# Filter rows of two groups loaded ahead into the space of matrices that are done with, in a spectral-filter kernel on Trainium2

**Chip, cores, metric.** One core of a Trainium2 chip; different calls used different chips. The metric is the device time of one execution in microseconds (us), median of several runs. All times "at 41.72" are microseconds from the start of the profiled execution's span.

## The reference, cut to what matters

```python
# x: 2048 x 1024 bf16; w_r, w_i: 2048 x 513 bf16 (the filter, real and imaginary part)
def _A_ref(x, w_r, w_i):                       # spectral layer
    X = rfft2(x.astype(float32))
    X = X * (w_r + 1j * w_i)
    return irfft2(X, s=(S, D)).astype(bfloat16)

def _B_ref(x, w1, b1, w2): ...                 # feed-forward layer 1024 -> 3584 -> 1024, mish

x = x + _A_ref(_layernorm(x), A_w_r, A_w_i)    # the early loads touch only this line
x = x + _B_ref(_layernorm(x), B_w1, B_b1, B_w2)
x = x + _A_ref(_layernorm(x), A_w_r, A_w_i)
x = x + _B_ref(_layernorm(x), B_w1, B_b1, B_w2)
```

## The kernel before

The Fourier transforms are matmuls with DFT tables. The spectral layer runs in steps over 8 groups of rows (two halves each): a first step `s1` with scaled matrices, a second (`s2`) and third (`s3`) forward, two inverse ones (`i1`, `i2`), a round trip through memory (`u_turn`, `u_back`, `u_last`) that transposes, and a fifth step after it. The steps of different groups are interleaved by the list in `order_A` (a word such as `241` is step 2, group 4, half 1).

Before `s3` can multiply group g by the filter, that group's filter rows (512 KB: `w_r` and `w_i`, 256 KB each) must be in SBUF, and `filter_bins(g)` must have arranged them: four matmuls (L921) that mirror the bins, two VectorE copies (L932) and two ScalarE copies (L936). In the first spectral layer (`li == 0`) the rows lie in a ring `WR` of two buffers, so group g+2 may only be loaded when group g has been used up:

```python
self.o = dict(..., WR=54 * K, YS=96 * K, UT=64 * K, MN=64 * K, ...)   # bytes in each partition
# ... cut
def load_w(self, g):
    if self.li == 0:
        self.load_wr(self.WR[g % 2], g)
        return
# ... cut: the second layer reads back what the first has arranged
def load_wr(self, wr, g):
    wr.res.begin()                     # waits for all readers of what lay in the buffer
    a, b = slots_of(g)
    for c, src in enumerate((self.w_r, self.w_i)):
        rows = src.rearrange("(k s) d -> k s d", s=16)[:, a:b + 1:b - a, 1:513]
        self.dma(self.sp if g < 2 else self.pool, wr.ap[:, c, :, :], rows, ..., parts=[wr.res])
```

```python
self.s1(li)                            # reads the scaled matrices at offset MN
# ... cut: the rings of the later steps
self.UT = self.alloc("UT", o["UT"], [P, P])      # the transposed components, over the same space
self.r_ut = self.sub_res(self.UT, "ut", 4, o["UT"], P * P * 2)
for r in self.r_ut:
    r.begin()
for stage, g, h in self.order_A():
    if stage == 2:
        s2(g, h)
        if li == 0 and h == 0:
            filter_bins(g)
            if g < 6:
                load_w(g + 2)
    elif stage == 3:
        s3(g, h)
        if h:
            if g < 6:
                load_tabs(g + 2)       # forward table c_ft
            # ... cut
    elif stage == 4:
        i1(g, h)
        if h and g < 6:
            load_btabs(g + 2)          # inverse table c_bt
    else:
        i2(g, h)
        u_turn(g, h)
self.spin(26, 0)                       # filler matmuls while the round trip ends
```

`UT` and `MN` have the same offset: the scaled matrices are read for the last time in `s1`, and the transposed components arrive only when the first `u_back` runs, tens of microseconds later. In between, the space is empty, but it already belongs to `UT`.

## Time and profile before

| | before |
|---|---|
| median of 3 runs (lowest to highest) | 1017.54 us (1015.78 to 1019.77) |
| span of the profiled execution, granted clock | 1016.2 us, 0.998 |
| TensorE / ScalarE / VectorE busy over the span | 94% / 34% / 32% |
| stage touched: first second-step matmul to last inverse step | 39.67 to 105.20 us |

The averages over the span are mostly those of the feed-forward layers. What the change is worth is read in the stage alone, from the timelines of single engines: each line is start, length, engine, source line, operation and shapes, count, and in a bracket the idle time just before and what ended it. The prediction below shows most of these lines. The GpSimd timeline, with the issue of the `w_r` part for group 2 and for group 6:

```profile
41.72 0.77 POOL L249 DMA_DIRECT2D ARENA<-in_A_w_r_dram  x1 [3.97 <-PE PS L921]
...
68.72 0.71 POOL L249 DMA_DIRECT2D ARENA<-in_A_w_r_dram  x1 [7.01 <-PE PS L697]
```

The ScalarE timeline around TensorE's wait for group 2 (the line between these two, at 49.21, is in the prediction):

```profile
47.66 1.13 ACT L732 ACTIVATE ARENA<-PS 128x1024 bf16<-128x1024 f32 x1
...
50.07 1.02 ACT L749 ACTIVATE ARENA<-PS 128x1024 bf16<-128x1024 f32 x1
```

A transfer that nobody waits for costs nothing. The first GpSimd line is where group 2's rows are asked for, and the second is one that I call **the hinge**: everything that stands behind it in the GpSimd queue, above all the inverse table `c_bt`, starts no sooner.

### The profile page before, as it was taken

How to read it: one execution, taken by the hardware profiler on the slowest of the kernel's cores; microseconds unless marked ns; L12 is line 12 of the kernel's file. 1: busy time of each engine (PE TensorE's matmuls, PEld its weight loads, DVE VectorE, ACT ScalarE, POOL GpSimd, SP SyncE). 2: the span in 40 equal slices, each digit the busy share in tenths (PEclk: the TensorE clock that was granted, in tenths of full speed). 3: DMA queues.
4: the chain of work that ended last, by engine and by line, in shares of the span. 5: the costliest groups of instructions: out<-in, count | busy, mean ns of one | idle time of the engine just before them, and what ended most of it. 6: DMA issues, size and time to landing. Idle time of an engine off the chain costs nothing.

```text
span 1016.2 us, 13732 instructions
## 1 busy us (share of the span) xinstructions
PE 955.1 (94%) x5779; PEld 507.3 (50%) x5865; DVE 326.5 (32%) x679; ACT 347.3 (34%) x482; POOL 81.5 (8%) x114
## 2 busy tenths in 40 slices
PE   0799799999999999999999978999999999999998
PEld 0577575444444444444456757644444444444443
DVE  6797469002444000033347736830011100000111
ACT  7798384330000433300029847543100024330000
POOL 4651000000000000002511100000000000000000
PEclk9999999999999999999999999999999999999999
DMA  9979813562111220002932875246411212100000
GB/s 283 247 221 320 212 61 114 181 205 72 47 46 32 73 83 21 1 21 82 195 66 82 233 188 140 89 156 207 126 27 46 73 52 80 45 1 11 21 26 27
DMA packets 154205, 107.00 MB, mean 105 GB/s; under 512 B 74448, under 2 KB 133664, under 8 KB 154144
## 3 DMA queue, kind: packets, MB, share of 16 engines
q1 hardware_dynamic: 143056, 78.61, 27.3%
q0 software_dynamic: 8912, 25.84, 8.8%
q10 hardware_dynamic: 2176, 1.66, 0.5%
q8 instruction: 47, 0.77, 0.3%
q14 instruction: 14, 0.11, 0.0%
HBM read 80.85 MB, written 20.71 MB: 100 GB/s over the span
## 4 chain that ended last, share of the span: by engine, by line
PE 86%; DVE 4%; DMA 4%; ACT 4%; issue 1%; SPq 0%; POOL 0%; ACTq 0%; DVEq 0%; POOLq 0%
PE PS L1057 38%; PE PS L1040 37%; PE PS L771 2%; PE PS L697 2%; PE PS L792 2%; DMA ARENA<-c_bt 1%; PE PS L950 1%; ACT ARENA L441 1%; DMA ARENA<-u_scratch 1%; DVE ARENA L619 1%; DMA XS<-in_A_x_dram 1%; ACT ARENA L550 1%; PE PS L1006 1%; DVE ARENA L592 1%; PE PS L810 1%
## 5 line engine op out<-in xcount | busy, mean ns | idle before, releaser
L1040 PE MATMUL PS<-ARENA 128*128 128x512 bf16 (+1 forms) x1950 | 389.3, 358 | 2.5 <-DVE ARENA L1011 0.6
L1057 PE MATMUL PS<-ARENA 128*128 128x512 bf16 x1756 | 385.5, 379 | 1.9
L1044 ACT ACTIVATE ARENA<-PS,B 128x512 bf16<-128x512 f32 (+1 forms) x248 | 158.9, 645 | 410.9 <-PE PS L1040 410.6
L1040 PEld LDWEIGHTS PS<-ARENA 128*128 128x128 bf16 x1984 | 192.8, 98 | 193.8 <-DVE ARENA L1011 1.5
L1057 PEld LDWEIGHTS PS<-ARENA 128*128 128x128 bf16 x1792 | 175.4, 98 | 211.4
L1062 DVE TENSOR_TENSOR XS<-PS,XS 128x512 bf16<-128x512 f32 x64 | 44.2, 691 | 587.1 <-PE PS L1057 587.1
L460 DVE BATCH_NORM_STATS2 BN<-XS 128x6 f32<-128x512 bf16 x100 | 64.7, 675 | 6.2 <-DMA XS<-in_A_x_dram 5.0
L550 ACT ACTIVATE ARENA<-PS 128x1440 bf16<-128x1440 f32 (+3 forms) x26 | 28.0, 1095 | 28.0 <-DVE XS L972 24.4
L249 POOL DMA_DIRECT2D xn_scratch<-ARENA x12 | 6.5, 541 | 374.5 <-DVE ARENA L512 374.5
L771 PE MATMUL PS<-ARENA 128*128 128x256 bf16 x256 | 32.4, 273 | 4.1 <-DVE ARENA L760 3.2
L778 ACT ACTIVATE ARENA<-PS 128x1024 bf16<-128x1024 f32 x32 | 33.0, 1051 | 7.1 <-PE PS L771 7.1
L432 ACT ACTIVATE RS<-MV,EPS 128x2 f32<-128x2 f32 (+2 forms) x5 | 1.5, 298 | 96.8 <-DVE MV L463 96.2
L697 PE MATMUL PS<-FD,ARENA 128*128 128x256 bf16 (+1 forms) x256 | 31.8, 271 | 2.4 <-ACT ARENA L617 1.2
L749 ACT ACTIVATE ARENA<-PS 128x1024 bf16<-128x1024 f32 x32 | 32.5, 1044 | 4.5 <-PE PS L745 4.5
L771 PEld LDWEIGHTS PS<-ARENA 128*128 128x128 bf16 x256 | 24.2, 98 | 11.8 <-DVE ARENA L760 5.5
L753 DVE TENSOR_TENSOR ARENA<-ARENA 128x1024 bf16<-128x1024 bf16 x32 | 22.0, 688 | 20.4 <-ACT ARENA L749 20.3
L697 PEld LDWEIGHTS PS<-FD,ARENA 128*128 128x128 bf16 x256 | 24.4, 98 | 6.5 <-DVE ARENA L619 1.4
L820 ACT ACTIVATE ARENA<-PS 128x1024 bf16<-128x1024 f32 x26 | 26.7, 1063 | 2.4 <-PE PS L792 2.4
L792 PE MATMUL PS<-ARENA,BD 128*128 128x256 bf16 x192 | 24.9, 273 | 2.3 <-ACT ARENA L778 2.3
L950 PE MATMUL PS<-MT,ARENA 128*128 128x32 bf16 (+1 forms) x512 | 20.9, 195 | 4.5 <-DMA ARENA<-u_scratch 2.5
L512 DVE TENSOR_SCALAR ARENA<-XS,MV,RS 128x1024 bf16<-128x1024 bf16 x48 | 24.8, 542 | 1.0
L732 ACT ACTIVATE ARENA<-PS 128x1024 bf16<-128x1024 f32 x22 | 22.9, 1058 | 3.1 <-PE PS L697 3.1
(76 smaller groups left out, 515.5 us busy)
## 6 DMA issues: line engine op xcount, KB each, us to landing
ARENA<-in_B_w_dram SPq DMA_DIRECT2D x56, 512.0 KB, 3.9
ARENA<-in_B_w_dram SPq DMA_DIRECT2D x56, 256.0 KB, 4.1
u_scratch<-ARENA SPq DMA_DIRECT2D x14, 512.0 KB, 3.7
ARENA<-u_scratch SPq DMA_DIRECT2D x14, 512.0 KB, 6.1
w_scratch<-ARENA POOLq DMA_DIRECT2D x8, 512.0 KB, 6.2
ARENA<-w_scratch POOLq DMA_DIRECT2D x8, 512.0 KB, 5.4
out_dram<-XS SPq DMA_DIRECT2D x16, 256.0 KB, 2.0
ARENA<-xn_scratch POOLq DMA_DIRECT2D x15, 256.0 KB, 10.0
```

Of the source, the lines that this page charges most:

```text
L460: self.op(self.dve, lambda e: e.bn_stats(self.BN[:, j, 6 * h:6 * h + 6], self.XS[:, j, 512 * h:512 * h + 512]), reads=[self.r_xs[j]], part ...
L550: fn = (lambda e: e.activation(dst, src, ACT.Copy)) if scale is None else \
L697: fns.append(lambda e: e.matmul(dst, at(r), FD[:, t:t + n], start=start, stop=stop))
L749: self.op(act, lambda e: e.activation(x.ap.rearrange("p a b -> p (a b)"), ps, ACT.Copy, scale=SIG), reads=banks, writes=[x.res])
L771: fns.append(lambda e, c=c, part=part: e.matmul(ps[:, c * 256:(c + 1) * 256], yk.ap[:, part, c * P:(c + 1) * P], t[:, (128, 0)[part]:(384, ...
L778: self.op(act, lambda e: e.activation(v.ap[:, :, i, :], src, ACT.Copy), reads=banks, parts=[v.res])
L792: fns.append(lambda e, dst=dst, part=part, c=c: e.matmul(dst, BD[:, c:c + P], mov(kd, part), start=(part == 0), stop=(part == 1)))
L950: fns.append(lambda e, l=l: e.matmul(self.PS[:, bank + l // k, l % k * w:(l % k + 1) * w], self.UT.ap[:, u0 + l, :], self.MT[:, 8 * lo:8 * ...
L1040: fns.append(lambda e, db=db, bank=bank, fl=fl: e.matmul(PS[:, bank, 0:w], wb.ap[:, db, fl * P:(fl + 1) * P], x.ap[:, db, tok], start=(db ...
L1044: self.op(act, lambda e, bank=bank, ft=ft: e.activation(at.ap[:, ft, tok], PS[:, bank, 0:w], ACT.Mish, bias=self.B1[:, ft:ft + 1]), reads= ...
L1057: fns.append(lambda e, i=i, ft=ft: e.matmul(PS[:, bank, :], at.ap[:, ft, t * P:(t + 1) * P], W2[ft].ap[:, h * 512:(h + 1) * 512], start=(i ...
L1062: self.op(dve, lambda e: e.tensor_tensor(xs, PS[:, bank, :], xs, ALU.add), reads=[self.r_bank[bank]], writes=[self.r_xs[j]])
```

## The change

Its intent: use the empty space. Groups 2 and 3 get buffers `WX` of their own in the first 8 KB of it, so that their rows are loaded as soon as `s1` has finished; groups 4 and 5 then follow groups 0 and 1 in the ring, 6 and 7 follow 4 and 5. For that, `UT` is opened only at the first `u_back` (in the second spectral layer too, where nothing is loaded into the space).

```diff
+    def wr(self, g):
+        return self.WX[g - 2] if g in (2, 3) else self.WR[g % 2]
@@ load_w, filter_bins
-            self.load_wr(self.WR[g % 2], g)
+            self.load_wr(self.wr(g), g)
-            self.filter_bins(g, ps, banks, self.WR[g % 2], ...
+            self.filter_bins(g, ps, banks, self.wr(g), ...
@@ layer_A
+        def open_ut():
+            self.UT = self.alloc("UT", o["UT"], [P, P])
+            self.r_ut = self.sub_res(self.UT, "ut", 4, o["UT"], P * P * 2)
+            for r in self.r_ut:
+                r.begin()
         def u_back(g):
+            if self.UT is None:
+                open_ut()
@@ after s1
-        self.UT = self.alloc("UT", o["UT"], [P, P])
-        self.r_ut = self.sub_res(self.UT, "ut", 4, o["UT"], P * P * 2)
-        for r in self.r_ut:
-            r.begin()
+        self.UT = None
+        if li == 0:
+            self.WX = [self.alloc(f"WX{i}", o["UT"] + 4096 * i, [2, 2, 512]) for i in range(2)]
+            for g in (2, 3):
+                load_w(g)
@@ the loop, after filter_bins(g)
-                    if g < 6:
+                    if g in (0, 1):
+                        load_w(g + 4)
+                    elif g in (4, 5):
                         load_w(g + 2)
```

Source lines shift by it: L697, L732, L749, L771, L792, L921, L932 and L936 of before are L701, L736, L753, L775, L796, L936, L947 and L951 after. L936 is therefore ScalarE's copy before and TensorE's filter matmul after.

More of the change, by code (lines that the diff above doesn't have):

```diff
@@ L682, in filter_bins @@
             ps, banks, _ = self.pair()
-            self.filter_bins(g, ps, banks, self.WR[g % 2], WT[2 * g % 8:2 * g % 8 + 2], o["WT"] + 2048 * (2 * g % 8),
+            self.filter_bins(g, ps, banks, self.wr(g), WT[2 * g % 8:2 * g % 8 + 2], o["WT"] + 2048 * (2 * g % 8),
                              self.JT, self.r_jt, dve)
```

## The prediction

> **What bounds the kernel now.** I read the page first, then the chain of work that ended last in order of time, then the timeline of each engine in the stretch that the change touches, then busy times by stretch. The page's section 4 tells how little there is to win anywhere outside the two big matmul lines:
>
> ```profile
> PE 86%; DVE 4%; DMA 4%; ACT 4%; issue 1%; SPq 0%; POOL 0%; ACTq 0%; DVEq 0%; POOLq 0%
> PE PS L1057 38%; PE PS L1040 37%; PE PS L771 2%; PE PS L697 2%; PE PS L792 2%; DMA ARENA<-c_bt 1%; PE PS L950 1%; ACT ARENA L441 1%; DMA ARENA<-u_scratch 1%; DVE ARENA L619 1%; DMA XS<-in_A_x_dram 1%; ACT ARENA L550 1%; PE PS L1006 1%; DVE ARENA L592 1%; PE PS L810 1%
> ```
>
> Two matmul lines of the feed-forward layers hold 75% of the chain. The change touches only the first spectral layer, some 60 us of the 1016 (about 38.5 to 97 us). The chain in that stretch, in order of time (start, length, what):
>
> ```profile
> 41.72 0.76 POOL ARENA L249
> 42.48 5.94 DMA ARENA<-in_A_w_i_dram
> 48.42 0.14 issue
> 48.56 0.62 PE PS L921 x4
> ...
> 68.72 1.24 POOL ARENA L249 x2
> 69.96 0.19 issue
> 70.16 9.51 DMA ARENA<-c_bt
> 79.67 0.14 issue
> 79.81 1.03 PE PS L771 x8
> ```
>
> The first block is what the change aims at: the filter rows of group 2 are asked for at 41.72, once group 0 has let go of its buffer, and the last of them lands at 48.42; TensorE then begins group 2's filter matmuls (L921). The second block is a later pair of the same kind: a wait for an inverse table (c_bt), which stands in the GpSimd queue behind the filter load of group 6.
>
> A transfer of 5.94 us on the chain isn't 5.94 us to win. The timeline of TensorE says how long it really stood (the idle time is in the bracket):
>
> ```profile
> 48.56 0.62 PE L921 MATMUL PS<-ARENA 128*128 128x256 bf16 x4 [1.41 <-DMA ARENA<-in_A_w_i_dram]
> 76.31 0.62 PE L921 MATMUL PS<-ARENA 128*128 128x256 bf16 x4 [0.32 <-DMA ARENA<-in_A_w_i_dram]
> 79.81 1.03 PE L771 MATMUL PS<-ARENA 128*128 128x256 bf16 x8 [0.90 <-DMA ARENA<-c_bt]
> ```
>
> So 1.41 us at group 2, 0.32 at group 6 (the seventh L921 group), 0.90 at the table. The timeline of ScalarE, which empties most PSUM banks here, says what these waits meant to it:
>
> ```profile
> 49.21 0.87 ACT L936 ACTIVATE ARENA<-PS 128x384 bf16<-128x384 f32 x2 [0.42 <-PE PS L921]
> 69.49 1.02 ACT L732 ACTIVATE ARENA<-PS 128x1024 bf16<-128x1024 f32 x1 [0.23 <-PE PS L697]
> 71.68 1.94 ACT L749 ACTIVATE ARENA<-PS 128x1024 bf16<-128x1024 f32 x2 [0.40 <-PE PS L745]
> ```
>
> While TensorE stood 1.41 us, ScalarE stood only 0.42, because it was about a microsecond behind. After that it does not stop for 20 us. Busy times of PE, PEld, DVE, ACT and POOL in that stretch, with counts, then clock, DMA share and GB/s:
>
> ```profile
> 49.20:69.40 20.20, 20.10 (x175) 15.38 (x176) 18.87 (x35) 20.02 (x25) 7.92 (x13) 1.00 0.65 221
> ```
>
> ScalarE 20.02 of 20.20 us, VectorE 18.87, TensorE 20.10: three engines run out together, and the clock is full. That decides what removing a TensorE wait is worth.
>
> **What the Trainium skill says.** "Perfetto Trace Analysis", section "Identifying the Most-Contended Engine", takes occupancy as a fair measure for Scalar and Vector but not for matmul time. The trace agrees on what matters: ScalarE at 99% is a real bound here. "DMA: Bandwidth & Descriptors", section "Issuing engines are not separate DMA queues", says that transfers from all issuing engines interleave on the same 16 DMA engines; so an early load is in competition with the tables that the SyncE queue is bringing in. The trace shows that stretch crowded: 250 GB/s and a DMA share of 1.09 between 40 and 48.5 us. "SBUF — State Buffer", section "SBUF: two separate sides", warns that a GpSimd-issued DMA can be starved of descriptors while VectorE runs a two-port copy. Here the six GpSimd-issued real-part loads take 0.70 to 0.77 us to issue, one of them beside the L932 copy; one c_bt issue beside L932 took 0.92 instead of 0.54. So that effect is 0.4 us at most.
>
> **The change, part by part.**
>
> (1) Groups 2 and 3 get their own buffers in the first 8 KB of the space of the first (scaled) matrices, which the first stage's matmuls have finished with. Their four loads are placed in the GpSimd queue before anything else of this stage, and wait only for the last matmul of the first stage, which ends at 38.51 (start 37.90 plus 0.61). GpSimd is free from 37.75 (32.16 plus 5.59). So the two loads of group 2 issue at about 38.6 and 39.3, in place of 41.72 and 42.48: 3.1 us earlier. With the measured 5.9 us to landing the last would land at 45.3, with 8 us (crowding) at 47.3. TensorE reaches the place at 47.15 (48.56 less 1.41), and ScalarE could not take the result before 48.79 (L732, 47.66 plus 1.13). TensorE needs about 0.65 us from load to result (48.56 to 49.21), so a landing up to about 48.0 costs ScalarE nothing. The wait goes from the bound engine even if a little of it remains on TensorE. Gain there: 0.42 us on ScalarE, 1.41 on TensorE.
>
> (2) Does the 0.42 survive? VectorE stood 0.35 us for ScalarE at 53.88 and 0.43 at 63.03. Between, it is fully busy (53.88 to 62.60). If ScalarE comes 0.42 earlier, VectorE begins at 53.53, is done at 62.25, and takes the next L749 result at 62.98 less 0.42 = 62.56. So it follows by 0.4, and its copies for group 4 (67.04 to 68.43) end 0.4 earlier.
>
> (3) Those copies are the hinge. They free the buffer into which group 6 is loaded, and the load and the c_bt behind it start at 68.72 and 70.16. The order of the GpSimd queue from there on is the same in both kernels. So group 6's rows and the table land 0.4 earlier, no more: TensorE gets the table at 79.4 instead of 79.81. TensorE and ScalarE may gain another 0.23 and 0.40 in between (the brackets at 69.49 and 71.68), but they hand it back as a longer wait for group 6 and for c_bt. The 1.41 of TensorE thus becomes 0.4 at 79.8.
>
> (4) From there the layer is a chain through its last transfers into the feed-forward layer, all relative to each other, so 0.4 passes through to the end.
>
> (5) Groups 4 and 5 are now loaded at about 41.7 and 43.7 instead of 51.8 and 57.6. They were never waited for (needed at 65.1 and 69.3): 0. The tables queued behind these loads move ahead of them between 46 and 60 us; nobody waited for those either: 0.
>
> (6) The transposed components' buffer opened at first use: it must only wait for what lay in its space, long read by then. The comparison of instruction orders shows the SyncE queue and ScalarE unchanged, waits included, and on TensorE and VectorE only another semaphore's name at the filter waits. Cost 0 in the first spectral layer and in the second.
>
> Sum: 0 to 0.5 us, central 0.4; 1017.54 less 0.4 is 1017.1.
>
> **The rivals.**
>
> A. TensorE is the bound, and every bracket counts: 1.41 at group 2, and the 0.32 at group 6 too: 1.7 us, 1015.8. For it: TensorE is back to back from 48.56 to 75.8. Against: ScalarE's 0.42, and the hinge in (3), which TensorE's lead does not move.
>
> B. The queue behind also clears up, and the c_bt wait goes as well: 1.41 plus 0.32 plus 0.90 is 2.6 us, 1014.9. Against: its issue stays behind group 6's load, which still waits for group 4.
>
> C. The early loads crowd out what is needed first. Half a megabyte for each of four groups now moves between 38.6 and 48 us, twice as much as before. The first forward table lands at 41.2 (34.79 plus 6.4) and is needed at 43.5, so it has 2.3 us; group 1's rows landed at 40.7 (34.28 plus 6.4), needed by TensorE at 42.5, so 1.8 us; group 2's table was in at 50.0 and is needed at about 54. If the pressure eats more than that, a new wait takes the place of the old one: no gain, or up to 1 us of loss, 1017.5 to 1018.5.
>
> **Range and chances.** Main line 55%, A and B together 15%, C 30%; all of them lie within 1014.9 and 1018.5. The spread of the three runs before, 1015.78 to 1019.77, is larger than any of them: the median of three new runs can be off by over a microsecond. Range 1014.8 to 1019.2. Two per cent is 20 us, while all waits of TensorE here together are 2.6: faster 0.01, slower 0.01.
>
> **What would show it right or wrong.** In the changed profile: group 2's loads issued near 38.6 to 40 us; no bracket, or under 0.5 us, at the third L921 group; ScalarE without its 0.42 there; group 6's load issued at about 68.3 instead of 68.7; the c_bt bracket still there and longer than 0.9, and likewise that of group 6. If the c_bt bracket is gone and the stage ends over a microsecond earlier, A or B was right, and step (3) is wrong. If TensorE or ScalarE shows a new wait for a forward table or for group 1's rows before 50 us, C was right. The spectral stage's own times, not the total, must decide, since the total's noise is larger.

## The result, and the profile after

| | before | after |
|---|---|---|
| median, same chip and rounds | 1016.79 us (4 runs, 1015.78 to 1019.77) | 1017.65 us (4 runs, 1016.26 to 1018.69) |
| five rounds, another chip | 1018.09 us (11 runs, 1016.31 to 1019.95) | 1016.66 us (6 runs, 1016.03 to 1021.47) |
| span of the first profiled execution, clock | 1016.2 us, 0.998 | 1015.7 us, 0.998 |
| TensorE's wait at the third filter group | 1.41 us | none |
| first second-step matmul to the hinge | 29.05 us | 28.30 us |
| the same to the last `i2` group | 65.53 us | 64.60 us |
| the same to the first fifth-step group | 74.74 us | 73.81 us |

After over before is 1.0003 with an interval from 0.9978 to 1.0028; in the five rounds it is 1.0000, from 0.9981 to 1.0018. Both say "same", and both intervals are wider than anything that this stage can give: 0.1% is 1.0 us. So the total can't decide; the stage's own distances can. I count them from the first second-step matmul (L697, L701 after), at 39.67 us before and 39.97 after, because that point itself moves by over a microsecond between executions with what comes ahead of it.

Now the lines after. The page's shares of the chain that ended last have hardly moved:

```profile
PE 85%; DVE 6%; ACT 4%; DMA 3%; issue 1%; SPq 0%; ACTq 0%; POOL 0%; DVEq 0%
```

The GpSimd timeline after: group 2's two loads, right after the first stage's last matmul, and the hinge.

```profile
39.11 0.76 POOL L249 DMA_DIRECT2D ARENA<-in_A_w_r_dram  x1 [1.05 <-PE PS L611]
39.87 0.73 POOL L249 DMA_DIRECT2D ARENA<-in_A_w_i_dram  x1
...
68.27 0.71 POOL L249 DMA_DIRECT2D ARENA<-in_A_w_r_dram  x1 [8.70 <-PE PS L701]
```

The loads start 2.6 us earlier (2.9 counted from the second step), the hinge 0.45 us earlier (0.75 counted from the second step). The TensorE timeline after: the third filter group without a bracket, a wait that is new, and the two waits that follow the hinge.

```profile
47.28 0.62 PE L936 MATMUL PS<-ARENA 128*128 128x256 bf16 x4
...
60.35 0.39 PE L746 MATMUL PS<-ARENA 128*128 128x512 bf16 x1 [0.45 <-DVE ARENA L738]
...
76.10 0.62 PE L936 MATMUL PS<-ARENA 128*128 128x256 bf16 x4 [0.52 <-ACT ARENA L782]
...
79.17 1.03 PE L775 MATMUL PS<-ARENA 128*128 128x256 bf16 x8 [0.49 <-DMA ARENA<-c_bt]
```

So 1.41 us of waiting has gone; 0.45 us came back at 60.35, where VectorE had yet to empty a PSUM bank, the wait at group 6 is 0.52 instead of 0.32, and the table's wait fell from 0.90 to 0.49. The ScalarE timeline after, at the same place as the two lines shown of before, and a line from later in the same row with the start of the next one:

```profile
47.95 1.14 ACT L736 ACTIVATE ARENA<-PS 128x1024 bf16<-128x1024 f32 x1
48.86 1.00 ACT L951 ACTIVATE ARENA<-PS 128x384 bf16<-128x384 f32 x2
49.60 1.18 ACT L753 ACTIVATE ARENA<-PS 128x1024 bf16<-128x1024 f32 x1
...
59.37 1.34 ACT L782 ACTIVATE ARENA<-PS 128x1024 bf16<-128x1024 f32 x1
60.27 1.35 ACT L824 ACTIVATE ARENA<-PS 128x1024 bf16<-128x1024 f32 x1
```

ScalarE no longer stands. But look at the starts, not at the bracket. Before, from the instruction at 47.66 to the one at 50.07 it took 2.41 us; after, the same two are 1.65 us apart (47.95 to 49.60). The difference is **0.76 us, though the bracket said 0.42**. Most of the reason is in the lengths: the instruction at 47.66 is reported as 1.13 us long, but the same one in an undisturbed row is followed 0.91 us after its start (47.95 to 48.86). In a row without a stop the reported lengths grow while the distance of the starts doesn't: 1.14 us at 47.95, 1.34 at 59.37, and still 0.90 us to the next start. So the tail of a reported length, 0.22 us here, hides part of the stall behind it. The other 0.12 us is lost behind the bracket: the two copies at 49.21 held ScalarE for 0.86 us (to 50.07), in the undisturbed row for 0.74 (48.86 to 49.60). The Trainium skill, "ScalarE: Activation LUTs", section "What ACT_TABLE_LOAD costs", says that back-to-back ScalarE instructions overlap by about 93 ns; the trace agrees for a row that has just begun (0.10 us: 1.02 long at 50.07 before, the next at 50.99) and has up to 0.44 late in a row.

The busy time by stretch (PE, PEld, DVE, ACT, POOL with counts, clock, DMA share, GB/s) fits this: ScalarE has no idle time that TensorE's gain could use, and VectorE hardly any:

```profile
48.50:60.00 11.50, 11.29 (x92) 7.97 (x92) 11.36 (x22) 11.50 (x16) 2.67 (x5) 1.00 0.73 281
```

Last, the chain of waits after, around the hinge. It has the same shape as before, with the table's flight 9.34 instead of 9.51 us:

```profile
68.27 1.28 POOL ARENA L249 x2
...
69.70 9.34 DMA ARENA<-c_bt
79.04 0.14 issue
79.17 1.03 PE PS L775 x8
```

### The profile page after: what moved, and what is told of

The parts are those of the page before. It is cut to its first block, busy times and chain, and to the rows that moved or that the text cites. A ratio compares the mean times of both kernels' runs of the same rounds, so it can differ in the third digit from the quotient of the medians.

```text
span 1015.7 us, 13730 instructions
## 1 busy us (share of the span) xinstructions
PE 956.3 (94%) x5779; PEld 507.3 (50%) x5865; DVE 327.0 (32%) x679; ACT 346.9 (34%) x482; POOL 81.9 (8%) x114
## 4 chain that ended last, share of the span: by engine, by line
PE 85%; DVE 6%; ACT 4%; DMA 3%; issue 1%; SPq 0%; ACTq 0%; POOL 0%; DVEq 0%
PE PS L1072 38%; PE PS L1055 37%; PE PS L775 2%; PE PS L701 2%; PE PS L796 2%; PE PS L965 1%; DMA ARENA<-c_bt 1%; ACT ARENA L441 1%; DVE ARENA L619 1%; DMA XS<-in_A_x_dram 1%; ACT ARENA L550 1%; PE PS L1021 1%; DVE ARENA L592 1%; PE PS L814 1%; ACT ARENA L782 1%
## 5 line engine op out<-in xcount | busy, mean ns | idle before, releaser
L782 ACT ACTIVATE ARENA<-PS 128x1024 bf16<-128x1024 f32 x32 | 34.0, 1084 | 6.7 <-PE PS L775 6.7
L775 PE MATMUL PS<-ARENA 128*128 128x256 bf16 x256 | 32.4, 273 | 3.7 <-DVE ARENA L764 3.2
L753 ACT ACTIVATE ARENA<-PS 128x1024 bf16<-128x1024 f32 x32 | 33.4, 1075 | 4.5 <-PE PS L749 4.5
L701 PE MATMUL PS<-FD,ARENA 128*128 128x256 bf16 (+1 forms) x256 | 31.8, 271 | 2.4 <-ACT ARENA L617 1.2
L775 PEld LDWEIGHTS PS<-ARENA 128*128 128x128 bf16 x256 | 24.0, 98 | 11.8 <-DVE ARENA L764 5.5
L824 ACT ACTIVATE ARENA<-PS 128x1024 bf16<-128x1024 f32 x26 | 27.4, 1089 | 3.3 <-PE PS L796 3.2
L796 PE MATMUL PS<-ARENA,BD 128*128 128x256 bf16 x192 | 26.2, 282 | 2.3 <-ACT ARENA L782 2.3
L701 PEld LDWEIGHTS PS<-FD,ARENA 128*128 128x128 bf16 x256 | 24.4, 98 | 6.5 <-DVE ARENA L619 1.4
L736 ACT ACTIVATE ARENA<-PS 128x1024 bf16<-128x1024 f32 x22 | 23.4, 1079 | 3.2 <-PE PS L701 3.2
```

Source lines behind the costliest of these rows:

```text
L701: fns.append(lambda e: e.matmul(dst, at(r), FD[:, t:t + n], start=start, stop=stop))
L753: self.op(act, lambda e: e.activation(x.ap.rearrange("p a b -> p (a b)"), ps, ACT.Copy, scale=SIG), reads=banks, writes=[x.res])
L775: fns.append(lambda e, c=c, part=part: e.matmul(ps[:, c * 256:(c + 1) * 256], yk.ap[:, part, c * P:(c + 1) * P], t[:, (128, 0)[part]:(384, ...
L782: self.op(act, lambda e: e.activation(v.ap[:, :, i, :], src, ACT.Copy), reads=banks, parts=[v.res])
L796: fns.append(lambda e, dst=dst, part=part, c=c: e.matmul(dst, BD[:, c:c + P], mov(kd, part), start=(part == 0), stop=(part == 1)))
```

## The experiments

Twelve runs were made. Nine gave one execution each beside one of the kernel before, so their state is unknown and I compare only distances inside their traces; three had five rounds. **Theory**: what counts is not TensorE's wait but the part of it that ScalarE's backlog can't absorb, and this part passes by way of VectorE to the hinge and to the end. **Rivals**: (N) the difference between two profiles is chance; (U) opening `UT` late does it; (A) all of TensorE's wait counts; (C) the earlier loads push something else back.

### The kernel before again, the kernel after again

No edit.

> The kernel before, unchanged, profiled once more, to see how far the stage's own clock repeats. Measure: from the first second-step matmul (39.67 us in the first profile) to the first matmul of the long filler group at the stage's end (108.79), 69.12 us. Theory (the stage is a fixed chain, and the 0.93 us between the two profiles is the change): 69.1 within 0.2, brackets again near 1.4 (third filter group) and 0.9 (c_bt). Rival (0.9 us is profile noise): the distance moves by 0.5 us or more.

> The changed kernel, unchanged, profiled once more. Same measure, 68.19 us in its first profile. Theory: 68.2 within 0.2, no bracket at the third filter group, c_bt bracket near 0.5. Rival (noise): moves by 0.5 us or more towards 69.1.

The kernel before, executed again, on the TensorE timeline:

```profile
47.43 0.62 PE L921 MATMUL PS<-ARENA 128*128 128x256 bf16 x4 [0.46 <-DMA ARENA<-in_A_w_i_dram]
```

The wait was 0.46 us instead of 1.41, because the rows landed 5.0 us after their issue instead of 5.9; the hinge stood at 28.30, the last `i2` group at 64.54 us: **this execution of the old kernel lost nothing**. The kernel after gave 28.30 and 64.59 again. So rival N holds in part: what the change removes varies from execution to execution, and one profile of the kernel before oversells it. My expectation of 69.1 us to the fillers was missed (68.13); the rival's came true. In its place the changed kernel has something constant: its hinge stood at 28.30, 28.30 and 28.29 us in three profiles.

The second profile of the kernel after also brought a surprise: the clock granted to TensorE fell to 0.50 at the end of the stage, and the first filler matmul came 69.57 us after the second step instead of 68.19, so this expectation was missed too. More on this below.

### UT opened late, loads as before

```diff
 # before, with only this:
-        self.UT = self.alloc("UT", ...); ...   # after s1
+        self.UT = None
         def u_back(g):
+            if self.UT is None:
+                open_ut()
```

> The kernel before with the second part of the change alone: the transposed components' buffer is opened at its first use, no early loads. Theory: this part does nothing: stage distance 69.1 within 0.2, both brackets as before. Rival: a late opening loosens or adds a wait of the SyncE queue, and the distance moves by over 0.3 us.

```profile
49.27 0.62 PE L926 MATMUL PS<-ARENA 128*128 128x256 bf16 x4 [1.19 <-DMA ARENA<-in_A_w_i_dram]
```

The wait is there, 1.19 us, and the hinge stands at 28.84 us: a loss of 0.54 us against 28.30. The fillers came after 68.59 us, not within 0.2 of 69.1 as expected, and by the letter of the expectation that was the rival's sign. But the two executions of the old kernel themselves lie at 69.12 and 68.13, and the loss at the hinge is the one that this run's own wait asks for, by the line of the next experiment. So nothing is left for rival U: no effect of opening `UT` late shows; it only makes room.

### A wait made longer

Three profiles with the old loads now gave waits of 0.46, 1.19 and 1.41 us, and losses at the hinge of 0, 0.54 and 0.75 us. That is a line: loss = wait less 0.65 us, and none below. To test it on a point that it had not been made from, I delayed group 2's load with a memset of the buffer it goes into:

```diff
 # before, with:
                     if g < 6:
+                        if g == 0:
+                            self.op(pool, lambda e, w=self.WR[0].ap: e.memset(w, 0.0), writes=[self.WR[0].res])
                         load_w(g + 2)
```

> The kernel before with one GpSimd memset of group 0's freed filter buffer ahead of group 2's load, so that this load lands later by the memset's length (some 1 to 2 us). Theory (of TensorE's wait at the third filter group, ScalarE's backlog hides 0.65 us and the rest goes through to group 6's load, whose distance from the first second-step matmul is 28.30 us when nothing is lost): with a bracket of w, this distance is 28.30 + w - 0.65, within 0.15 us; for w = 2.5, 30.15. Rival 1 (the whole wait counts): 28.30 + w. Rival 2 (the idle bracket of ScalarE is what counts): 28.30 plus that bracket.

GpSimd, TensorE and ScalarE timelines, one line or two of each:

```profile
42.39 2.05 POOL L870 MEMSET ARENA<- 128x2048 bf16 x1 [3.52 <-DVE ARENA L934]
...
70.20 0.71 POOL L249 DMA_DIRECT2D ARENA<-in_A_w_r_dram  x1 [7.02 <-PE PS L697]
```

```profile
50.04 0.62 PE L923 MATMUL PS<-ARENA 128*128 128x256 bf16 x4 [1.78 <-ACT ARENA L732]
```

```profile
50.69 0.87 ACT L938 ACTIVATE ARENA<-PS 128x384 bf16<-128x384 f32 x2 [0.78 <-PE PS L923]
```

The wait was 1.78 us, so the line asks for a hinge at 28.30 + 1.78 - 0.65 = 29.43; measured 70.20 - 40.78 = **29.42**. The rivals asked for 30.08 (the whole wait) and 29.08 (ScalarE's bracket). Note the ScalarE bracket: 0.78, for a loss of 1.12, once more 0.34 short. (TensorE's bracket names a ScalarE copy, which ended at 49.91; the load landed at about 49.9 too, 4.4 us after its issue at 45.49. By the kernel's order these matmuls use a PSUM bank that an earlier copy had emptied by 47.16, so it was the load.)

Where the 0.65 us come from can be read in the kernel after. There ScalarE takes up the third filter group 1.58 us after TensorE starts it (47.28 to 48.86); where it has nothing else to do, it takes 0.65 (48.56 to 49.21 before). So it is 0.93 us behind. Of this, 0.12 us go for the restart after a stall (above), and another 0.17 because TensorE's bracket understates too: from start to start, the wait of 1.41 is one of 1.58 us (8.89 us after the second step instead of 7.31). 0.93 - 0.12 - 0.17 = 0.64.

### The same with the bound engines relieved

Is it ScalarE's backlog that absorbs the 0.65 us? Take the backlog away and every bit of the wait must count. I cut ScalarE's copy in the third step and VectorE's four products to half width, in both kernels, with TensorE's work unchanged. Their outputs are wrong, which doesn't matter for the times.

```diff
 # before and after, both with (third step, L749 to L760; i1 then reads the written half twice):
-  act: x.ap (1024 columns)             <- ps
+  act: x.ap[:, :, 0:256] (512 columns) <- ps
-  dve: ta, tb, yk at 512 columns of each part
+  dve: ta, tb, yk at 256 columns of each part
```

> Wrong results on purpose: the kernel before, with the third step's PSUM copies on ScalarE and its four products on VectorE cut to half their width (TensorE's matmuls stay as they are), so that TensorE alone sets the pace. Read together with its partner, the changed kernel cut in the same way. Measure: from the first second-step matmul to the issue of group 6's filter load (the hinge), 28.30 us in both profiles of the changed kernel, 29.05, 28.30 and 28.84 in the three with the old loads, whose bracket at the third filter group was 1.41, 0.46 and 1.19. Theory (ScalarE's backlog hides the first 0.65 us of TensorE's wait, since 1.41 cost 0.75, 1.19 cost 0.54 and 0.46 cost nothing): with the backlog gone the whole wait costs: hinge of this kernel less hinge of its partner equals its bracket within 0.25 us. Rival (the hinge hides it for another reason): bracket less 0.65 still.

> Wrong results on purpose: the changed kernel cut in the same way as light_before. Theory: no bracket at the third filter group, hinge earlier than 28.30 because TensorE sets the pace, and earlier than light_before's by that one's whole bracket (within 0.25). Rival: earlier by the bracket less 0.65.

The pair's kernel before, on the TensorE and on the GpSimd timeline, and below each line the same place in its partner:

```profile
48.32 0.61 PE L921 MATMUL PS<-ARENA 128*128 128x256 bf16 x4 [1.11 <-ACT ARENA L732]
46.68 0.62 PE L936 MATMUL PS<-ARENA 128*128 128x256 bf16 x4
```

```profile
66.41 0.71 POOL L249 DMA_DIRECT2D ARENA<-in_A_w_r_dram  x1 [6.09 <-DVE ARENA L932]
64.78 0.71 POOL L249 DMA_DIRECT2D ARENA<-in_A_w_r_dram  x1 [6.09 <-DVE ARENA L947]
```

Here the hinge moved from 26.67 to 25.42 us, by 1.25 for a wait of 1.11: all of it counts. (From start to start the wait is 1.26 us: 8.58 us after the second step, 7.32 in the partner.) With the backlog, the line would have given 1.11 - 0.65 = 0.46. So **the absorber is the work that ScalarE and VectorE have queued**, and it is gone when they are relieved. It is one pair of single profiles, and it relieves both engines at once, so it doesn't say which of the two counts. The second line settles another question. In the kernel before, the hinge's bracket names a TensorE line (L697), while the prediction took VectorE's copies of group 4 for the releaser. Here VectorE is named, and the matmuls in question begin only at 67.31, after the issue. In every profile that I looked at, the issue follows the end of these copies by 0.28 to 0.30 us. The copies are the hinge.

### The wait for the inverse table taken away

After the hinge TensorE still waits for `c_bt`, since its load stands behind group 6's. I moved that one load ahead of it:

```diff
 # after, with:
+                    if g == 4:
+                        load_btabs(4)
                     ...load_w(g + 2)
-                if h and g < 6:
+                if h and g < 6 and not (li == 0 and g == 2):
                     load_btabs(g + 2)
```

> The changed kernel, with the inverse table of group 4 put ahead of group 6's filter load in the GpSimd queue. Theory (the hinge: c_bt lands late because it stands behind a load that waits for group 4's copies): c_bt issues near 60 us in place of 69.7, its bracket (0.49) goes, and the stage gets shorter by 0.3 to 0.6 us, to 67.6 to 67.9. Rival 1 (something else sets the same place, the group 6 filter wait or ScalarE): bracket gone, distance within 0.15 of 68.2. Rival 2 (the 9.3 us to landing is crowding and not queue position): the table still lands late.

The table's wait is gone, and there is none at group 6 ahead of it: the last `i2` group came at 63.59 instead of 64.60 us, 1.0 us and more than expected. Both waits count there: in the three profiles of the kernel after, these two brackets sum to 1.01, 0.98 and 0.61 us, and the last `i2` group comes 1.01, 1.00 and 0.72 us later than here. But the third of them has no wait at group 6 either, so that this edit takes that one away is not shown. Still, the first fifth-step group came at 74.08 us, not at 72.8. The chain of waits shows where it was handed back (store to memory, read back, fifth step):

```profile
107.75 2.41 DMA u_scratch<-ARENA
110.17 0.02 issue
110.19 4.48 DMA ARENA<-u_scratch
114.67 0.24 issue
114.91 0.97 PE PS L967 x32
```

In the kernel after, in two of its three profiles, the fifth step begins as the fillers end; here the round trip through memory is what it waits for, 1.34 us beyond the fillers. The stage's end has a second bound just beside the first.

### More loaded early: three groups, four groups

If two groups ahead are good, are three or four better? In the first, groups 2 to 4 lie in the empty space and the ring serves 5 to 7, so that group 6 waits for group 1 instead of group 4 and the hinge is gone. In the second, group 5 is loaded ahead too, into a buffer of the round trip that isn't yet in use.

```diff
 # w6_early: after, with
-        return self.WX[g - 2] if g in (2, 3) else self.WR[g % 2]
+        return self.WX[g - 2] if g in (2, 3, 4) else self.WR[{0: 0, 1: 1, 5: 0, 6: 1, 7: 0}[g]]
-            for g in (2, 3):
+            for g in (2, 3, 4):
-                        load_w(g + 4)
-                    elif g in (4, 5):
+                        load_w(g + 5)
+                    elif g == 5:
                         load_w(g + 2)
 # all_early: after, with groups 2 to 5 loaded ahead (5 in the third U buffer), then load_w(g + 6) after groups 0 and 1
```

> The changed kernel with the loads of groups 2, 3 and 4 in the space of the first matrices and group 5 and 6 following groups 0 and 1, so that only group 7 waits for a late group; the table of group 4 is then no longer behind a waiting load. Measure: first second-step matmul to the last long group of fourth-step matmuls, 64.60 and 64.59 in the changed kernel, 63.59 with the table moved ahead. Theory (hinge): c_bt and the group 6 brackets both gone, 63.2 to 63.6. Rival C (crowding by early loads): the forward table of group 2, 0.6 us later in the queue or more, lands after 53.4 us and TensorE waits for it; no gain over 64.6.

> All six late filter loads at once: groups 2 to 4 in the space of the first matrices, group 5 in a buffer of the components' ring not yet in use, 6 and 7 right after groups 0 and 1. 12 loads of 256 KB are asked for before group 2's forward table, which should issue about 2.9 us later than in the changed kernel (45.7), at about 48.6. Rival C (crowding) is put to the test on purpose: with 6.5 us to landing the table is there at about 55 where it is needed at 53.4, a new bracket of 1 to 2 us there, of which less than all gets through because of the backlog; measure as in w6_early 63.3 to 64.5. If no bracket for the table shows up, crowding was never near.

With three groups no wait for rows or tables is left: last `i2` group at 63.27 us, 1.3 us sooner than after. With four, the TensorE timeline has this:

```profile
54.02 0.38 PE L746 MATMUL PS<-ARENA 128*128 128x512 bf16 x1 [1.09 <-DMA ARENA<-c_ft]
```

That is rival C, real at this size: the forward table was issued behind all those loads and landed too late. It was its place in the queue: it was asked for 2.8 us later than in the kernel after (8.48 us after the second step, not 5.69), and took no longer to land (6.1 us, there 6.5). Its 1.09 us made the last `i2` group 0.39 us later than with three groups, near the line's 1.09 - 0.65 = 0.44. The Trainium skill, "DMA: Bandwidth & Descriptors", section "Rules for kernel authors", advises to issue a transfer early and to wait for it late; here this holds for one transfer, but what is issued early stands ahead of another in the same queue.

In both kernels, though, the fillers began only at 68.43 and 68.72 us, no sooner than after's 68.19: the clock fell again at the stage's end.

### Five rounds, and fillers against the clock's fall

To see whether the 1.3 us reach the total, I timed the kernel after, the three-group kernel, and the latter with a few filler matmuls (results unused) in the gaps of TensorE at the end of the stage:

```diff
 # w6_warm: w6_early, with, for the first layer:
+                if g == 7: self.spin(3 if h == 0 else 4, free bank)     # ahead of i1(7, h)
                 i1(g, h)
+                if (g, h) == (7, 0): self.spin(4, free bank)            # ahead of i2(7, 0)
                 i2(g, h)
```

> The changed kernel, timed against the kernel before in five rounds. Theory: the stage is 0 to 1.0 us shorter, depending on how late the old load lands in a given run (65.53, 64.54 and 65.00 in the three profiles with old loads, 64.60 and 64.59 with the new); expected ratio 0.9995, interval a few tenths of a per cent, so same. Rival: a real loss that the profiles don't show, ratio 1.001 or more with the interval clear of 1.

> w6_early again, timed in five rounds. Its stage measure was 63.27, so 1.3 us less than the changed kernel and 1.3 to 2.3 less than the kernel before. Theory: 1.3 to 2.0 us faster than before, ratio 0.998 to 0.9987, if the gain isn't given back; against it stands that in w6_early the granted clock fell to 0.50 in 103 to 105 us and the stage's last matmuls took 5.2 us in place of 3.6, which gave 1.6 us back. Rival: this clock dip comes often with the shorter stage and the ratio is within 0.0005 of 1.

> w6_early with 3, 4 and 4 filler matmuls ahead of the last three waiting groups of the stage (group 7's inverse steps), into the bank that the next group will write, so that TensorE isn't idle there. Theory (the dip comes from the low activity of TensorE between 98 and 105 us): the granted clock stays 1.00 through that place, the distance from the last long fourth-step group to the filler group at the stage's end is 3.6 us and not 5.2, stage measure 63.3 within 0.3, and the time at or below that of w6_timed, on average by 0.5 us. Rival: the fillers delay the groups behind them by more than 0.3 us, or the clock dips all the same.

Busy times by stretch at the end of the stage, of the three-group kernel without fillers (columns as before; the clock is the third number from the end):

```profile
101.00:103.00 2.00, 1.05 (x8) 0.70 (x8) 0.00 (x0) 1.02 (x2) 0.00 (x0) 1.00 1.04 243
103.00:105.00 2.00, 1.81 (x9) 1.31 (x10) 0.00 (x0) 0.14 (x1) 0.00 (x0) 0.52 1.20 229
```

and with them:

```profile
101.00:103.00 2.00, 1.69 (x12) 1.10 (x12) 0.03 (x1) 0.98 (x2) 0.00 (x0) 1.00 1.05 249
103.00:105.00 2.00, 1.75 (x18) 1.22 (x18) 0.00 (x0) 0.86 (x2) 0.00 (x0) 1.00 1.14 219
```

Without fillers TensorE is half idle in the first stretch, in gaps of up to 1.12 us; then the clock is halved for 3.4 us, and the group that took 1.48 us takes this:

```profile
103.19 2.74 PE L796 MATMUL PS<-ARENA,BD 128*128 128x256 bf16 x12 [1.12 <-ACT ARENA L782]
```

With fillers the clock stayed full and the last fillers began at 66.85 us, 1.55 us sooner than without. But the fifth step came at 74.05 us, against 75.73 without fillers, 73.61 in the kernel after and 73.81 in its first profile. Once more the round trip took it: the store to memory took 3.45 us instead of 2.41 in the table experiment, and the reads back went out 70.30 us after the second step, as in the kernel after (70.25). Crowded DMA engines don't explain the long store: while it ran (106.80 to 110.25) the mean DMA share was 0.44, against 0.74 during the shorter one (107.75 to 110.17 in the table experiment). The mean doesn't exclude single slow engines; the cause stays open.

The totals: after over before 1.0000 (0.9981 to 1.0018), three groups 0.9997 (0.9981 to 1.0012), with fillers 0.9992 (0.9979 to 1.0005; median 1017.27 us, five runs). The expectation for three groups, 0.998 to 0.9987, was missed; the rival's, within 0.0005 of 1, came true. Nothing beats the kernel before by more than the intervals.

At this place, the end of the first spectral layer, the halved clock was seen in the profiles of `after_again`, `late_load`, `w6_early`, `w6_timed` and `all_early`, in 5 of 11 profiles of full kernels without the added fillers, not in those of `before`, `before_again`, `ut_only`, `after`, `after_timed` and `bt4_early`. One kernel has it in one execution and not in the other (the kernel after: 68.19 and 67.90 us to the fillers without, 69.57 with). It is worth some 1.4 us at the fillers, and the fifth step came 76.29 us after the second step instead of 73.81 and 73.61. One case is a kernel with the old loads, so the change alone isn't the cause.

The clock falls elsewhere too. Of all 14 profiles, 11 have such a fall between 594 and 616 us, in the second spectral layer (`before` from 608.9 to 612.9), three a further one between 116 and 122 us (the relieved pair one between 112 and 119), and only `ut_only` has none. The mean clock of a run counts them: it was 1.000 in the profile with none, 0.998 in those with one, 0.996 or 0.997 with two, 0.994 with three. By this count, in the five rounds, 2 of 11 runs of the kernel before had more than one fall, 3 of 6 of the kernel after, 4 of 6 with three groups, and 2 of 5 with the fillers, these two at 0.997. So the falls may well be more frequent in the kernels with early loads; the runs are too few to tell, and one profile with fillers can't show that these prevent the fall.

The Trainium skill, "TensorE: Matmul & The Clock Gate", section "Part 1: The HAM clock gate", tells of such a halving after an idle window of some 3.4 us that runs freely against the kernel. The length of the fall agrees with it; but no gap ahead of the fall shown was longer than 1.12 us, so it seems that a half-busy window can be enough.

## Why the prediction was right, point by point

The time (1017.65 us, predicted 1017.1, range 1014.8 to 1019.2) and "same" were right; with such noise the total would have allowed much. The steps are the real test:

- **Step 1**, mechanism right, size not. The loads issued at 39.11 and 39.87 (predicted 38.6 and 39.3; the first stage ended 0.3 us later in that execution), the last landed at about 46.2 (predicted 45.3 to 47.3), and TensorE's and ScalarE's brackets are gone. The term "0.42 on ScalarE" was mis-sized: it was read from a bracket, and the starts show 0.76 us for that execution. The law behind it is wait less 0.65 us; by it a landing up to about 47.7, not 48.0, costs ScalarE nothing. What saved the number 0.4 is luck, since the profile was an unlucky one: the three profiles with the old loads and an unchanged load time lost 0.75, 0.54 and 0, on average 0.43 us. The prediction had the right average for a wrong reason. Another size was wrong without cost: the delay of a GpSimd issue beside VectorE's copies, "0.4 us at most", was 0.75 us in the kernel after (the `w_r` part of group 3, at 40.59, took 1.47 us instead of 0.72, beside copies from 40.83 to 42.22).
- **Step 2** right: ScalarE's gain goes on through VectorE. The hinge moved by as much as ScalarE did (0.75 and 0.76 us).
- **Step 3** right in its core: group 4's copies are the hinge, shown by the relieved pair, and TensorE's lead from the wait is cut down to what they allow; most of this happened at 60.35 already. Wrong in a detail: the bracket at `c_bt` did not grow beyond 0.9; it was 0.49, 0.83 and 0.61 us in the three profiles, and that at group 6, forecast to grow from 0.32, was 0.52, 0.15 and none. I had let TensorE and ScalarE gain another 0.23 and 0.40 us in between, to be handed back there. They did not get them, ScalarE's brackets remained (0.27 and 0.40), so nothing was there to hand back.
- **Step 4** right as far as it can be followed: the gain is still whole at the fifth step (0.93 us between the first two profiles: 0.75, and 0.17 from a table that flew 9.34 instead of 9.51 us). Not foreseen: in some executions the halved clock takes more than all of it. Without those, the fifth step came after 74.74, 73.75 and 74.21 us with the old loads (mean 74.23) and 73.81 and 73.61 with the new (mean 73.71): 0.5 us. The first feed-forward matmul of these profiles came after 86.01, 84.49 and 84.95 us with the old loads, 84.55 and 84.58 with the new. That it reaches the kernel's end is not shown.
- **Steps 5 and 6** right: no new wait for groups 4 and 5 or their tables, and no effect of opening `UT` late shows (the run with that alone).
- **Rivals.** A falls with the full backlog and holds without it (the relieved pair), which is the best proof of the theory. B falls: the table's wait stayed. C did not occur in the changed kernel, and appeared with twice as many groups loaded ahead.

Open: why the round trip took up to a microsecond longer when it began sooner, what decides whether the clock falls, and whether it falls more often with the early loads.

## What to carry to other kernels

A wait of one engine is worth what is left of it after the backlog of the engine behind it, and the backlog is measured by start-to-start times, not by idle brackets. Before trusting a wait in one profile, take a second one: a transfer that lands just in time in one execution is a microsecond late in the next, and loading it earlier may buy constancy rather than speed. Where a stage ends in a round trip through memory, a gain ahead of it can be lost there, so measure behind it.

## What the Trainium skill lacked or had wrong

- "ScalarE: Activation LUTs", section "What ACT_TABLE_LOAD costs", gives an overlap of about 93 ns for instructions in a row. The runs show 0.10 us at the start of a row, but up to 0.44 late in one: reported lengths of the same 128x1024 copy grow from 1.02 to 1.34 us at an unchanged distance of 0.90 us. The page has nothing on this growth, nor on what it does to an idle bracket, which understated ScalarE's loss by 0.34 us (0.42 for 0.76, 0.78 for 1.12).
- "TensorE: Matmul & The Clock Gate", section "Why this matters for your kernels", warns of idle gaps over about 3 us. The runs show the clock at 0.50 to 0.52 for 3.4 us with no gap over 1.12 us ahead of it, where TensorE had been about half busy, and only in 5 of 11 profiles at that place. The page tells elsewhere of one kernel whose short idle times made the clock swing, but gives no length or busy share for it.
- "DMA: Bandwidth & Descriptors", section "Anatomy of one DMA — SWDGE (gpsimd) path", has a fit of about 2.0 us plus the bytes over 436e3, which is an estimate of 2.6 us for 256 KB. In this crowded stage the same load took 5.0 and 5.9 us in two executions of one kernel, and a table took 9.34 and 9.51 us. The page has no measured time for such a load among others, nor for its spread.
